# Linear attention and two mixture layers on one core: the first batch's copies, the router's end and the second batch's first unit in another order

## The chip, the core and the metric

The kernel runs on one core of a Trainium2 chip. The core's engines each work through their own list of instructions in order: PE (matrix products), DVE (vector), ACT (activations and copies), POOL (GpSimd), and SP, which issues the transfers (DMAs) and loads a register. An instruction starts when its engine has finished the ones ahead of it in the list and when the results that it needs are there. The metric is the device time of one execution in microseconds (us); lower is better.

## What is computed

```python
q_s = exp(q - max(q, -1));  q_s /= sum(q_s, -1) + 1e-9        # q, k, v: [8 batches, 8 heads, 576 tokens, 64]
k_s = exp(k - max(k, 2));   k_s /= sum(k_s, 2) + 1e-9
x = einsum('bhsd,bhde->bhse', q_s, einsum('bhsd,bhse->bhde', k_s, v))   # then [4608 tokens, 512]
e_idx = argmax(x @ w_gate, 1)                                 # 8 experts
gate = max softmax probability of x @ w_gate
eom = sigmoid(x @ w_output_gate)
for e in range(8):                                            # tokens of expert e
    x2[mask] = gate * eom[:, e] * (relu(x[mask] @ w1[e]) @ w2[e])       # 512 -> 1024 -> 512
h = max(x2 @ m_w1, x2 @ m_w2, x2 @ m_w3)                      # 512 -> 768
out = h @ m_wo
```

## The kernel before

A **unit** is half a batch: four heads of one batch, loaded as k, q and v. Units 0 and 1 are batch 0, units 2 and 3 batch 1, and so on. For a unit the stages are, by the names of the functions: `k_max` (DVE reduces k over a partition's five rows to `kmx`), `k_tr` (PE transposes `kmx` to `kT`; DVE makes `m` and the diagonal `dg`), `k_exp` (PE spreads the maxima to `kB`, DVE subtracts them from `k`, ACT takes the exponential into `ke`), `q_max` (DVE, `qm`), `q_exp` (DVE subtracts, ACT exponential), `q_sum` (DVE: sum `qs`, plus 1e-9, reciprocal), `kv_mm` (PE, k^T v, 20 small products), `kv_norm` (DVE, into `kvraw`, and a store), `q_norm` (DVE, into `qn`), then for each of the unit's two pairs of heads `q_tr` (PE transposes `qn` to `qT`, ACT copies it to `qTf`), `x_mm` (PE, `xT`, copied to `xr` and rounded to the high part in `xs`), `x_lo` (DVE, the low part of `xs`) and `logit_mm` (the router's products, `lgT`).

After a batch's two units the router runs: `logit_tr` and `route_1` choose an expert per token, `route_2` counts and finds the batch's most frequent expert, whose number SP loads into a register; `route_3` makes the tokens' gates; `route_4` and `route_5` make the table of the tokens that belong to other experts. With the number in the register `load_piece` issues the load of that expert's weights: the first piece in four quarters. `split_sub` (ACT) and `split_lo` (DVE for the first two weight tiles, then POOL) split each weight tile into a high and a low part.

The batch then passes through the expert as a whole in 32 **groups**, one per slot: `l1_group` (12 matmuls of 128x288 into `hp`, from `xs` and `w`; ACT writes the high part of `h`, DVE the low part) and `l2_group` (`yp`, from `h` and `w`). Four PSUM buffers (`ps_mm`) hold the groups' results.

The order of everything on every engine is that in which Python emits it. `first` is a list of calls for batch 0 (and some of unit 2, by `in_2`), put in slots -120 and up. From then on `moe_slot` emits a slot's group and then the calls that stand in `events` for that slot. For unit 2 and 3 the slots stand in `EARLY`: ten numbers for `k_max`'s stages in the order of `FRONT` (`None`: not there), and five for each pair in the order of `BACK`; `LOAD` holds the slot in which a unit's loads are issued. Slot 0 has batch 0's first group.

Of the kernel before, what the change touches and what calls it, by code (L numbers as in the profile page):

```python
# [9 lines left out]
F32 = mybir.dt.float32  # L10
F32R = mybir.dt.float32r
I32 = mybir.dt.int32
U32 = mybir.dt.uint32
ACTF = mybir.ActivationFunctionType
# [5 lines left out]
B, H, S, D = 8, 8, 576, 64  # L20
# [8 lines left out]
HF = S // 2  # L29
# [17 lines left out]

STEADY = ((-4, -1, -4, 0, 1, 3, 6, 6, 7, 8), (10, 10, 13, 14, 15), (15, 16, 17, 18, 19))
EARLY = {
    2: ((None, None, None, -8, -5, -3, 0, 0, 3, -1), (2, 3, 3, 7, 5), (5, 6, 7, 8, 9)),  # L50
    3: ((0, 3, 3, 5, 6, 6, 8, 8, 8, 9), (10, 10, 11, 13, 15), (13, 13, 14, 15, 16)),
}
LOAD = {3: -7, 4: 0, 5: 8}
ROUTE = (20, 22)
ROUTE0 = (7, 9)
ROUTE1 = (17, 19)
# [6 lines left out]
def tile_linear_attention__then__moe(  # L63
# [15 lines left out]
    nc = tc.nc  # L79
    dma = nc.sync.dma_start  # L80
    gdma = nc.gpsimd.dma_start
    vec = nc.vector
    act = nc.scalar.activation
# [6 lines left out]
    ident = const.tile([128, 128], F32, name="ident")  # L90
# [33 lines left out]
    x_po = es_x.enter_context(tc.tile_pool(name="x_po", bufs=4))  # L124
    x_pe = es_xe.enter_context(tc.tile_pool(name="x_pe", bufs=4))
# [9 lines left out]
    ps_at = es_att.enter_context(tc.tile_pool(name="ps_at", bufs=1, space=PSUM, side="right"))  # L135
# [49 lines left out]
    units = {}  # L185
    xp = {}
# [55 lines left out]
    def q_inv(b, hb):  # L242
        s = units[b, hb]["qs"]
        vec.tensor_scalar(out=s, in0=s, scalar1=1e-9, scalar2=None, op0=ALU.add)
        vec.reciprocal(out=s, in_=s)

    def q_max(b, hb):
        u = units[b, hb]
        qt = u["q"].rearrange("p h c d -> p (h c) d")
        m = sm.tile([128, 20, 1], F32, tag="qm", name="qm")  # L250
        vec.tensor_reduce(out=m[:, :, 0], in_=qt, axis=AX.X, op=ALU.max)
        u["qm"] = m
# [114 lines left out]
    def x_mm(b, hb, pr):  # L367
        u = units[b, hb]
        g = 2 * hb + pr
        if b == 0:  # L370
            ps = [ps_mm.tile([128, HF], F32, tag="mm", name="xT0") for i in range(2)]
        else:
            big = ps_at.tile([128, 2, 512], F32, tag="big", name="xT")
            ps = [big[:, i, 0:HF] for i in range(2)]
        qT = u["qT", pr]
        for i in range(2):
            cs = slice(HF * i, HF * i + HF)
            if b < NFULL:
                mm(ps[i], kvraw[hb][:, pr], qT[:, 0, cs], start=True, stop=True)
                continue  # L380
            kv = u["kv"]
            for n, (a, c) in enumerate(((0, 0), (0, 1), (1, 0))):
                mm(ps[i], kv[:, a, pr], qT[:, c, cs], start=(n == 0), stop=(n == 2))
        xr = u["xr", pr] = xr_p.tile([128, S], F32, tag="xr", name="xr")
        if b == 0:
            for i in range(2):
                act(out=xr[:, HF * i:HF * i + HF], in_=ps[i], func=ACTF.Copy)
            if hb == 1:
                return
        else:  # L390
            act(out=xr.rearrange("p (a t) -> p a t", a=2), in_=big[:, :, 0:HF], func=ACTF.Copy)
        t = xp[b, g] = (x_po if b % 2 else x_pe).tile([128, 2, S], F32R, tag="x", name="xs")
        act(out=t[:, 0], in_=xr, func=ACTF.Copy)

    def x_lo(b, hb, pr):
        xr = units[b, hb]["xr", pr]
        if b == 0 and hb == 1:
            t = xp[b, 2 * hb + pr] = (x_po if b % 2 else x_pe).tile([128, 2, S], F32R, tag="x", name="xs")
            act(out=t[:, 0], in_=xr, func=ACTF.Copy)
        t = xp[b, 2 * hb + pr]  # L400
        vec.tensor_tensor(out=t[:, 1], in0=xr, in1=t[:, 0].bitcast(F32), op=ALU.subtract)

# [124 lines left out]
    def at(slot, f, *args):  # L527
        events.setdefault(slot, []).append((f, args))
# [4 lines left out]
    def in_2(b, f):  # L533
        f(1, 0)

    first = (
        (load_k, 0), (load_k, 1), (load_q, 0), (load_v, 0), (load_q, 1), (load_v, 1),
        (k_max, 0), (k_tr, 0), (k_max, 1), (k_exp, 0), (k_tr, 1), (q_max, 0), (k_exp, 1), (q_exp, 0),
        (kv_mm, 0), (q_max, 1), (q_sum, 0), (kv_mm, 1), (q_norm, 0), (q_exp, 1), (kv_norm, 0), (q_tr, 0, 0), (kv_lo, 0),
        (load_2,), (q_sum, 1), (q_lo, 0, 0), (q_tr, 0, 1), (x_mm, 0, 0), (kv_norm, 1), (q_lo, 0, 1), (kv_lo, 1),  # L540
        (q_norm, 1), (q_tr, 1, 0), (x_mm, 0, 1), (logit_mm, 0, 0), (q_tr, 1, 1), (x_mm, 1, 0), (logit_mm, 0, 1),
        (x_mm, 1, 1), (x_lo, 0, 0), (x_lo, 0, 1), (logit_mm, 1, 0), (logit_mm, 1, 1), (in_2, q_max), (in_2, k_max),
        (logit_tr,), (route_1,), (route_2,), (in_2, q_exp), (x_lo, 1, 0), (x_lo, 1, 1), (route_3,),
    )
    for i, (f, *a) in enumerate(first):
        at(-120 + i, f, 0, *a)
    at(ROUTE0[0], route_4, 0)
    for c in range(5):
        at(ROUTE0[1] + 2 * c, route_5, 0, c)
    START = {n: 16 * n - 51 for n in range(2, 2 * B)}  # L550
    FRONT = (q_max, q_exp, k_max, k_tr, k_exp, q_sum, kv_mm, kv_norm, kv_lo, q_norm)
    BACK = (q_tr, q_lo, x_mm, x_lo, logit_mm)
    for n, s0 in START.items():
        b, hb = divmod(n, 2)
        if n in EARLY:
            t, s0 = EARLY[n], 0
        else:
            t = STEADY
        if n > 2:
            at(LOAD.get(n, START.get(n - 2, 0) + 9), load_unit, b, hb)  # L560
        for d, f in zip(t[0], FRONT):
# [347 lines left out]
    with tc.manual_schedule():  # L909
# [55 lines left out]
        def out_ps(nm):  # L965
            return ps_o.tile([128, 512], F32, tag="o", name=nm)
# [135 lines left out]
        def fx_kv(b_reg):  # L1102
            kv = fx_p.tile([128, 2, 2, 128], F32, tag="fkv", name="fkv")
            dma(out=kv, in_=kv_d[bass.ds(b_reg, 1)].rearrange("b a p g d -> p (b a) g d"))
            return kv

        def fx_x(kv, qT, qs):
            ps = out_ps("fx")
            for g in range(4):
                mm(ps[:, SLOT * g:SLOT * g + SLOT], kv[:, g // 2, g % 2], qT[:, g, qs], start=True, stop=True)  # L1110
            pv = ps[:, 0:4 * SLOT].rearrange("p (g t) -> p g t", g=4)
            x = fx_p.tile([128, 4, 2, SLOT], F32R, tag="fxs", name="fxs")
            act(out=x[:, :, 0], in_=pv, func=ACTF.Copy)
            vec.tensor_tensor(out=x[:, :, 1], in0=pv, in1=x[:, :, 0].bitcast(F32), op=ALU.subtract)
            return x
# [252 lines left out]
        for c in range(6):  # L1368
# [31 lines left out]
            for i in range(2):  # L1400
                col, x = tiles[i]
# [8 lines left out]
            for i, (col, x) in enumerate(tiles):  # L1410
                m = CAP if x is None else 128
                if i < 2:
                    ps = o[i]
                else:
                    ps = out_ps("op")
# [16 lines left out]
    with tc.For_i(0, n_trip, 1) as it:  # L1432
# [9 lines left out]
        ps = out_ps("lqT")  # L1442
# [6 lines left out]
        x = fx_x(fx_kv(b_reg), qT, slice(0, SLOT))  # L1449
        hh = []  # L1450
        y = None
        for i in range(4):
            ps = out_ps("lm")
# [11 lines left out]
        for f in range(6):  # L1465
# [11 lines left out]
            t = lp.tile([128, SLOT], F32, tag="ltm", name="ltm")  # L1477
# [7 lines left out]
        ps = out_ps("lo")  # L1485
# [40 lines left out]
```

## Time and profile before

| what | value |
|---|---|
| median of three runs | 1200.14 us (1200.04, 1200.14, 1201.42) |
| the profiled execution, its own time | 1197.52 us |
| its span, from the first instruction to the last | 1195.5 us |
| mean granted TensorE clock over the span | 0.986 of full |
| PE busy 45 to 50 us / 50 to 55 us / 55 to 60 us | 0.00 / 4.49 / 5.00 us |
| DVE busy 45 to 50 us / 50 to 55 us / 55 to 60 us | 3.24 / 4.19 / 4.82 us |

The span lies 2.0 us below the execution's own time, and that time lies 2.6 us below the median. PE is busy for 95% of the span; the first expert matmul begins near 50 us. A stretch's clock of 1.00 is 2.4 GHz, of 0.50 it is 1.2 GHz.

### The profile page before, as it was taken

To read this page: it belongs to the slowest core of one execution; us is meant where nothing else is said; L and a number is where in the kernel's file an instruction comes from. 1 tells how busy PE (TensorE), PEld (TensorE's weight loads), DVE (VectorE), ACT (ScalarE), POOL (GpSimd) and SP (SyncE) were. 2 spreads that over 40 slices of the span, in tenths; PEclk is the share of its full clock that TensorE was granted. 3 is DMA by queue.
4 is the path that set the end of the run, shared out by engine and by line. 5 is a ranking of instruction groups with operands and counts; after the bars stand their busy time and mean duration, and the time that the engine had idled before them with its cause. 6 is when DMAs were issued, how large, how long until landed. Compare 5 with 4: busy or idle time off the path is not lost. (4 is left out here: it accounts for less than half of the span.)

```text
span 1195.5 us, 21865 instructions
## 1 busy us (share of the span) xinstructions
PE 1136.8 (95%) x7626; PEld 1061.4 (89%) x7626; DVE 786.4 (66%) x1476; ACT 583.8 (49%) x1549; POOL 412.9 (35%) x502
## 2 busy tenths in 40 slices
PE   4699999999999999999999999999999999999994
PEld 2499899898999999999998899899899989989983
DVE  7777878788787878647798566455556446554430
ACT  2466676756667676536454423443344244333220
POOL 2156857677676857787241020000000000000000
PEclk8799999999999999999999999999999999999997
DMA  6784657576565654437698478487678848747701
GB/s 160 187 226 127 195 156 212 156 221 201 160 193 165 187 143 153 135 137 249 212 320 298 160 236 287 134 295 237 225 231 266 272 147 287 237 138 235 222 19 42
DMA packets 204210, 234.97 MB, mean 197 GB/s; under 512 B 78253, under 2 KB 122061, under 8 KB 204096
## 3 DMA queue, kind: packets, MB, share of 16 engines
q1 hardware_dynamic: 202384, 233.14, 62.7%
q8 instruction: 62, 1.02, 0.4%
q0 software_dynamic: 1712, 0.39, 0.2%
q14 instruction: 52, 0.43, 0.1%
HBM read 189.56 MB, written 44.13 MB: 195 GB/s over the span
## 5 line engine op out<-in xcount | busy, mean ns | idle before, releaser
L668 PE MATMUL yp<-h,w 128*128 128x288 f32 x1536 | 222.7, 299 | 7.4 <-DVE h L656 7.4
L668 PEld LDWEIGHTS yp<-h,w 128*128 128x128 f32 x1536 | 207.7, 188 | 11.4 <-DVE h L656 8.8
L650 PE MATMUL hp<-xs,w 128*128 128x288 f32 x1536 | 217.5, 298 | 0.0
L650 PEld LDWEIGHTS hp<-xs,w 128*128 128x128 f32 x1536 | 206.9, 188 | 2.6
L634 POOL TENSOR_TENSOR w<-stg,w 128x512 fp32r<-128x512 f32 x126 | 180.3, 1436 | 79.6 <-ACT w L627 78.1
L1248 PE MATMUL pY<-t,sw 128*128 128x384 f32 (+1 forms) x972 | 193.5, 342 | 2.1 <-ACT s L1257 1.7
L1248 PEld LDWEIGHTS pY<-t,sw 128*128 128x128 f32 x972 | 172.8, 188 | 6.3 <-ACT s L1257 2.9
L1225 POOL DMA_INDIRECT out_dram<-ocx,ftb x1 | 1.0, 981 | 481.8 <-SPq L1432 481.8
L1336 PE MATMUL op<-wo,hc 128*128 128x512 f32 (+1 forms) x666 | 156.2, 394 | 0.0
L1336 PEld LDWEIGHTS op<-wo,hc 128*128 128x128 f32 (+1 forms) x666 | 125.1, 188 | 27.9
L1257 ACT ACTIVATE s<-pY 128x384 f32<-128x384 f32 (+1 forms) x108 | 53.6, 496 | 133.5 <-PE pY L1248 129.6
L656 DVE SCALAR_TENSOR_TENSOR h<-hp,h 128x288 fp32r<-128x288 f32 x128 | 57.2, 453 | 64.3 <-ACT h L655 62.3
L240 ACT ACTIVATE q<-q,qm 128x64 f32<-128x64 f32 x240 | 80.1, 337 | 0.0
L627 ACT ACTIVATE w<-stg 128x512 fp32r<-128x512 f32 x128 | 78.9, 621 | 0.0
L655 ACT ACTIVATE h<-hp 128x288 fp32r<-128x288 f32 x128 | 50.9, 398 | 40.7 <-PE hp L650 40.5
L1264 ACT ACTIVATE hc<-c 128x384 fp32r<-128x384 f32 (+1 forms) x72 | 38.2, 530 | 62.2 <-DVE c L1287 61.8
L1248 PE MATMUL pZ<-B,sw 128*128 128x384 f32 (+1 forms) x324 | 66.8, 341 | 1.5 <-DVE c L1281 1.5
L1248 PE MATMUL pY<-B,sw 128*128 128x384 f32 (+1 forms) x324 | 66.4, 340 | 0.6 <-DVE y L675 0.6
L1248 PE MATMUL pX<-B,sw 128*128 128x384 f32 (+1 forms) x324 | 66.8, 341 | 0.0
L1248 PE MATMUL pX<-t,sw 128*128 128x384 f32 (+1 forms) x324 | 66.5, 340 | 0.0
L1248 PEld LDWEIGHTS pZ<-B,sw 128*128 128x128 f32 x324 | 57.9, 188 | 3.6 <-DVE c L1281 1.8
L1257 ACT ACTIVATE sx<-pX 128x384 f32<-128x384 f32 (+1 forms) x54 | 26.9, 497 | 67.6 <-PE pX L1248 64.2
(251 smaller groups left out, 1858.7 us busy)
## 6 DMA issues: line engine op xcount, KB each, us to landing
sw<-ws_d SPq DMA_DIRECT2D x315, 256.0 KB, 3.6
stg<-in_moe_w_dram SPq DMA_DIRECT2D x31, 1024.0 KB, 5.3
ws_d<-sw SPq DMA_DIRECT2D x63, 256.0 KB, 3.2
fw<-in_moe_w_dram SPq DMA_DIRECT2D x48, 256.0 KB, 4.1
v<-in_v_dram SPq DMA_DIRECT2D x80, 128.0 KB, 4.7
draw<-in_moe_w_dram SPq DMA_DIRECT2D x24, 384.0 KB, 4.8
k<-in_k_dram SPq DMA_DIRECT2D x16, 512.0 KB, 5.5
q<-in_q_dram SPq DMA_DIRECT2D x16, 512.0 KB, 6.8
```

The source lines that it names most:

```text
L240: act(out=qt[:, i], in_=qt[:, i], func=ACTF.Exp, bias=u["qm"][:, i], accum_out=u["qs"][:, i])
L627: act(out=t[:, 0], in_=src, func=ACTF.Copy)
L634: eng.tensor_tensor(out=t[:, 1], in0=src, in1=t[:, 0].bitcast(F32), op=ALU.subtract)
L650: mm(ps, w[:, a, kk], xp[b, kk][:, c, cs], start=(n == 0), stop=(n == 11))
L655: act(out=h[:, 0, cs], in_=ps, func=ACTF.Relu)
L656: vec.scalar_tensor_tensor(out=h[:, 1, cs], in0=ps, scalar=0.0, in1=h[:, 0, cs].bitcast(F32), op0=ALU.max, op1=ALU.subtract,)
L668: mm(ps, w[:, a, f], ht[f][:, c, cs], start=(n == 0), stop=(n == 11))
L1225: nc.gpsimd.indirect_dma_start(out=out[:, :], out_offset=bass.IndirectOffsetOnAxis(ap=tb[0:n, 0:1], axis=0), in_=src, in_offset=None, boun ...
L1248: mm(ps[:, 0:nn], w[:, a, kap], tt_[key, kap][:, cc, 0:nn], start=(start and k == 0), stop=(k == 5), skip_group_check=True)
L1257: act(out=t[:, 0:n_of(c)], in_=pst[n, "X" if nm == "sx" else "Y"][:, 0:n_of(c)], func=ACTF.Copy)
L1264: act(out=h[:, 0, cols], in_=t[:, 0:nn], func=ACTF.Copy)
L1336: mm(ps[0:m], hc[f][:, a, col:col + m], wo[f][:, cc], start=(f == F_ORDER[0] and i == 0), stop=(f == F_ORDER[5] and i == 2))
```

## The change

For batch 0, `x_mm` no longer makes the high part. A new function `x_hi` does: for unit 0 on POOL, for unit 1 on ACT behind `route_1`. For unit 1 the second half of `xr` is copied by DVE, the first by ACT. In `first`, unit 2's `q_max` stands in front of the low parts, `route_3` and `q_exp` of unit 2 leave the list, unit 2's `k_max` comes behind `route_2`, and `spin` puts 16 transposes of the identity matrix, read by nobody, on PE. `route_3` of batch 0 moves to slot 1. Unit 2's stages get other slots: `q_exp` -4, `k_tr` -6, `k_exp` 0, `q_sum` 1, `q_norm` 2, `kv_mm` and `kv_norm` 3, and its first pair's `q_tr` goes from slot 2 to 3. Unit 4's loads go from slot 0 to 3.

```diff
 EARLY = {
-    2: ((None, None, None, -8, -5, -3, 0, 0, 3, -1), (2, 3, 3, 7, 5), (5, 6, 7, 8, 9)),
+    2: ((None, -4, None, -6, 0, 1, 3, 3, 3, 2), (3, 3, 4, 7, 5), (5, 6, 7, 8, 9)),
-LOAD = {3: -7, 4: 0, 5: 8}
+LOAD = {3: -7, 4: 3, 5: 8}
...
+    def spin(b, n):
+        ps = ps_at.tile([128, 1024], F32, tag="big", name="spin")
+        for i in range(n):
+            nc.tensor.transpose(ps[:, 0:128], ident, ident)
...
             for i in range(2):
-                act(out=xr[:, HF * i:HF * i + HF], in_=ps[i], func=ACTF.Copy)
-            if hb == 1:
-                return
+                if i == 1 and hb == 1:
+                    vec.tensor_copy(xr[:, HF:S], ps[1])
+                else:
+                    act(out=xr[:, HF * i:HF * i + HF], in_=ps[i], func=ACTF.Copy)
+            return
...
+    def x_hi(b, hb, pr):
+        xr = units[b, hb]["xr", pr]
+        t = xp[b, 2 * hb + pr] = x_pe.tile([128, 2, S], F32R, tag="x", name="xs")
+        if hb == 0:
+            nc.gpsimd.tensor_copy(t[:, 0], xr)
+        else:
+            act(out=t[:, 0], in_=xr, func=ACTF.Copy)
...
-        (x_mm, 1, 1), (x_lo, 0, 0), (x_lo, 0, 1), (logit_mm, 1, 0), (logit_mm, 1, 1), (in_2, q_max), (in_2, k_max),
-        (logit_tr,), (route_1,), (route_2,), (in_2, q_exp), (x_lo, 1, 0), (x_lo, 1, 1), (route_3,),
+        (q_norm, 1), (in_2, q_max), (x_hi, 0, 0), (q_tr, 1, 0), (x_mm, 0, 1), (logit_mm, 0, 0), (x_lo, 0, 0),
+        (x_hi, 0, 1), (q_tr, 1, 1), (x_mm, 1, 0), (logit_mm, 0, 1), (x_lo, 0, 1), (x_mm, 1, 1),
+        (logit_mm, 1, 0), (logit_mm, 1, 1), (logit_tr,), (route_1,), (x_hi, 1, 0), (x_hi, 1, 1), (route_2,), (spin, 16),
+        (x_lo, 1, 0), (x_lo, 1, 1), (in_2, k_max),
...
+    at(1, route_3, 0)
```

Line numbers of the changed kernel are 6 to 15 higher than those of before for the same line. The first piece is DVE before, from the first weight tile of batch 0 on. In it `w` is a weight tile's low part, `k`, `qs`, `qn`, `kr` and `kvraw` are unit 2's, `h` is group 0's low part, and `qm` is unit 3's.

```order
L634 TENSOR_TENSOR w<-stg,w 128x512
L281 TENSOR_TENSOR k<-k,kB 128x1280
L634 TENSOR_TENSOR w<-stg,w 128x512
L289 TENSOR_REDUCE qs<-q 128x20
L290 TENSOR_SCALAR qs<-qs 128x20
L291 RECIPROCAL qs<-qs 128x20
L298 TENSOR_TENSOR qn<-q,qs 128x4x5x64
L656 SCALAR_TENSOR_TENSOR h<-hp,h 128x288
L325 TENSOR_SCALAR kr<-kv 128x2
L326 RECIPROCAL kr<-kr 128x2
L329 TENSOR_TENSOR kvraw_202<-kv,kr 64x2x64 x2
L251 TENSOR_REDUCE qm<-q 128x20
```

Unit 2's `qm` and `kmx` (ahead of the router), its subtraction `q` and the six instructions of `route_3` stand above this piece. Next is DVE in the changed kernel, from the low parts of unit 1's `xs` on; `kmx`, `m`, `dg`, `q` and `k` are unit 2's, `h` is group 0's, `qm` is unit 3's.

```order
L414 TENSOR_TENSOR xs<-xr,xs 128x576 x2
L224 TENSOR_REDUCE kmx<-k 128x256
L649 TENSOR_TENSOR w<-stg,w 128x512
L274 TENSOR_REDUCE m_567<-kT 128x2
L277 TENSOR_SCALAR dg<-ident,m_567 128x128 x2
L649 TENSOR_TENSOR w<-stg,w 128x512
L264 TENSOR_TENSOR q<-q,qm 128x1280
L671 SCALAR_TENSOR_TENSOR h<-hp,h 128x288
L287 TENSOR_TENSOR k<-k,kB 128x1280
L257 TENSOR_REDUCE qm<-q 128x20
```

Unit 2's `kmx` and `q` came in here, `h` of group 0 moved ahead of `k`, and unit 3's `qm`, which stood behind unit 2's `kvraw`, stands behind `k`. The rows that follow directly in the changed kernel, from group 1's `h` to unit 2's `qn`:

```order
L671 SCALAR_TENSOR_TENSOR h<-hp,h 128x288
L487 TENSOR_TENSOR rz<-roh,rl 128x40
L489 TENSOR_REDUCE rzs<-rz 128x5
L493 TENSOR_REDUCE rs<-rex 128x5
L494 TENSOR_SCALAR rs<-rs 128x5
L495 SCALAR_TENSOR_TENSOR rs<-rez,rs 128x5
L496 RECIPROCAL tsrc<-rs 128x5
L295 TENSOR_REDUCE qs<-q 128x20
L296 TENSOR_SCALAR qs<-qs 128x20
L297 RECIPROCAL qs<-qs 128x20
L671 SCALAR_TENSOR_TENSOR h<-hp,h 128x288
L304 TENSOR_TENSOR qn<-q,qs 128x4x5x64
```

`route_3` and the low parts of groups 1 and 2 have moved in front of unit 2's `qn`; between the second weight tile and `qn` there stood four instructions, now there stand fifteen. The next piece is PE before, where the expert's groups begin; `hp` x12 is one group, and `kT`, `kB`, `kv` and `qT` are unit 2's.

```order
L266 MATMUL kT<-ident,kmx 128x128 x2
L278 MATMUL kB<-dg,ones 128x256
L650 MATMUL hp<-xs,w 128x288 x12
L316 MATMUL kv<-v_199,ke 64x65 x20
L650 MATMUL hp<-xs,w 128x288 x24
L350 MATMUL qT<-ident,qn 128x128 x4
L351 MATMUL qT<-ident,qn 128x64
L650 MATMUL hp<-xs,w 128x288 x12
```

Here `kv` stands behind one group and `qT` behind three. The same place on PE in the changed kernel:

```order
L251 MATMUL spin<-ident 128x128 x16
L272 MATMUL kT<-ident,kmx 128x128 x2
L665 MATMUL hp<-xs,w 128x288 x12
L284 MATMUL kB<-dg,ones 128x256
L665 MATMUL hp<-xs,w 128x288 x36
L322 MATMUL kv<-v_199,ke 64x65 x20
L356 MATMUL qT<-ident,qn 128x128 x4
L357 MATMUL qT<-ident,qn 128x64
L665 MATMUL hp<-xs,w 128x288 x12
```

`kB` has moved behind group 0 and `kv` behind group 3; `qT`, which stood behind three groups, stands behind four. On SP's list nothing changes place.

## Rows read from the trace of the kernel before

**Rows 1.** Timeline, PE alone: start us, us, work [idle before it <-releaser].
```profile
24.97 1.11 PE L350 MATMUL qT<-ident,qn 128*128 128x128 f32 x4 [3.90 <-DVE qn L298]
...
50.05 1.19 PE L278 MATMUL kB<-dg,ones 128*128 128x256 f32 x2 [8.03 <-DVE dg L271]
50.67 2.98 PE L650 MATMUL hp<-xs,w 128*128 128x288 f32 x12
```

**Rows 2.** Windows: us, busy per engine (x instructions), granted clock, DMA share, GB/s.
```profile
52.50:53.00 0.50, 0.50 (x4) 0.50 (x4) 0.50 (x2) 0.20 (x1) 0.00 (x0) 0.53 1.06 385
```

**Rows 3.** Timeline, DVE alone.
```profile
27.36 0.17 DVE L290 TENSOR_SCALAR qs<-qs 128x20 f32<-128x20 f32 x1
...
36.65 2.36 DVE L224 TENSOR_REDUCE kmx<-k 128x256 f32<-128x1280 f32 x1
...
43.05 1.49 DVE L258 TENSOR_TENSOR q<-q,qm 128x1280 f32<-128x1280 f32 x1
46.44 1.43 DVE L401 TENSOR_TENSOR xs<-xr,xs 128x576 fp32r<-128x576 f32 x2 [1.91 <-ACT xs L399]
47.78 0.19 DVE L474 TENSOR_TENSOR rz<-roh,rl 128x40 f32<-128x40 f32 x1
...
49.00 0.38 DVE L268 TENSOR_REDUCE m<-kT 128x2 f32<-128x256 f32 x1
...
49.82 0.68 DVE L634 TENSOR_TENSOR w<-stg,w 128x512 fp32r<-128x512 f32 x1
51.27 1.49 DVE L281 TENSOR_TENSOR k<-k,kB 128x1280 f32<-128x1280 f32 x1 [0.77 <-PE kB L278]
...
53.28 1.48 DVE L289 TENSOR_REDUCE qs<-q 128x20 f32<-128x1280 f32 x1
54.79 1.18 DVE L290 TENSOR_SCALAR qs<-qs 128x20 f32<-128x20 f32 x1
...
56.32 2.21 DVE L298 TENSOR_TENSOR qn<-q,qs 128x1280 f32<-128x1280 f32 x1
...
59.82 1.49 DVE L251 TENSOR_REDUCE qm<-q 128x20 f32<-128x1280 f32 x1
61.34 1.37 DVE L656 SCALAR_TENSOR_TENSOR h<-hp,h 128x288 fp32r<-128x288 f32 x3
```

**Rows 4.** Timeline, ACT alone.
```profile
36.96 0.90 ACT L387 ACTIVATE xr<-xT 128x288 f32<-128x288 f32 x2 [0.72 <-PE xT L379]
...
44.57 1.27 ACT L259 ACTIVATE q<-q 128x1280 f32<-128x1280 f32 x1 [4.84 <-DVE q L258]
...
48.35 1.13 ACT L627 ACTIVATE w<-stg 128x512 fp32r<-128x512 f32 x2
```

**Rows 5.** Timeline, SP's DMA queue alone.
```profile
43.88 2.10 SPq L609 DMA_DIRECT2D stg<-in_moe_w_dram  x4
...
49.44 2.58 SPq L198 DMA_DIRECT2D q<-in_q_dram  x1
```

**Rows 6.** DMA issues at 27.4, 43.9, 49.4 us: KB each, us to landing.
```profile
q<-in_q_dram SPq DMA_DIRECT2D x1, 512.0 KB, 5.1
...
stg<-in_moe_w_dram SPq DMA_DIRECT2D x1, 256.0 KB, 2.7
...
q<-in_q_dram SPq DMA_DIRECT2D x1, 128.0 KB, 8.8
```

**Rows 7.** Timeline, PE alone, around the first qT of unit 2.
```profile
54.12 1.83 PE L316 MATMUL kv<-v,ke 128*64 128x65 f32 x40 [0.47 <-ACT ke L283]
55.88 3.45 PE L650 MATMUL hp<-xs,w 128*128 128x288 f32 x24
59.17 0.60 PE L350 MATMUL qT<-ident,qn 128*128 128x128 f32 x4
```

**Rows 8.** The page's groups by cost: busy, mean ns | idle before.
```profile
L668 PE MATMUL yp<-h,w 128*128 128x288 f32 x1536 | 222.7, 299 | 7.4 <-DVE h L656 7.4
...
L634 POOL TENSOR_TENSOR w<-stg,w 128x512 fp32r<-128x512 f32 x126 | 180.3, 1436 | 79.6 <-ACT w L627 78.1
```

More of the change, by code (lines that the diff above doesn't have):

```diff
@@ L393, in x_mm @@
         act(out=t[:, 0], in_=xr, func=ACTF.Copy)
+    def x_hi(b, hb, pr):
[5 more added lines that the diff above has]
+            act(out=t[:, 0], in_=xr, func=ACTF.Copy)
     def x_lo(b, hb, pr):
         xr = units[b, hb]["xr", pr]
-        if b == 0 and hb == 1:
-            t = xp[b, 2 * hb + pr] = (x_po if b % 2 else x_pe).tile([128, 2, S], F32R, tag="x", name="xs")
-            act(out=t[:, 0], in_=xr, func=ACTF.Copy)
         t = xp[b, 2 * hb + pr]
@@ L540, in tile_linear_attention__then__moe @@
         (load_2,), (q_sum, 1), (q_lo, 0, 0), (q_tr, 0, 1), (x_mm, 0, 0), (kv_norm, 1), (q_lo, 0, 1), (kv_lo, 1),
-        (q_norm, 1), (q_tr, 1, 0), (x_mm, 0, 1), (logit_mm, 0, 0), (q_tr, 1, 1), (x_mm, 1, 0), (logit_mm, 0, 1),
-        (x_mm, 1, 1), (x_lo, 0, 0), (x_lo, 0, 1), (logit_mm, 1, 0), (logit_mm, 1, 1), (in_2, q_max), (in_2, k_max),
-        (logit_tr,), (route_1,), (route_2,), (in_2, q_exp), (x_lo, 1, 0), (x_lo, 1, 1), (route_3,),
+        (q_norm, 1), (in_2, q_max), (x_hi, 0, 0), (q_tr, 1, 0), (x_mm, 0, 1), (logit_mm, 0, 0), (x_lo, 0, 0),
+        (x_hi, 0, 1), (q_tr, 1, 1), (x_mm, 1, 0), (logit_mm, 0, 1), (x_lo, 0, 1), (x_mm, 1, 1),
+        (logit_mm, 1, 0), (logit_mm, 1, 1), (logit_tr,), (route_1,), (x_hi, 1, 0), (x_hi, 1, 1), (route_2,), (spin, 16),
+        (x_lo, 1, 0), (x_lo, 1, 1), (in_2, k_max),
     )
```

## The prediction

> **What bounds the kernel now.** I read the page's busy shares first, then PE's waits, then the timelines of single engines in the stretch that the change touches. PE is the bound: once the expert's groups have started it hardly ever stands still. So the end moves by as much as PE's list is shifted in the first 70 us, unless something later takes the shift back. Before the groups, PE is idle for long stretches; the last ends when DVE delivers `dg`, after 8.03 us, and the first group then starts at 50.67 [rows 1]. Ahead of that DVE does unit 2's subtraction at 43.05, the low parts of unit 1's `xs` at 46.44 and `route_3` from 47.78 to 49.00, and only then `m`, `dg` and the first weight's low part at 49.82 [rows 3]. From group 0 on PE follows its list with short waits, and unit 2's first `qT` starts at 59.17, behind three groups [rows 7]. That `qT` is the place on which this forecast turns: PE can't pass it before DVE has written `qn`.
>
> **The change, part by part.**
>
> *The copies of batch 0.* ACT waited 0.72 us for PE before its last pair of `xr` copies [rows 4]: it was fed by PE, so its list being shorter gains nothing there. The second copy of that pair now runs on DVE, which could start no earlier than ACT did, since the half that it copies comes from PE last. A DVE copy of 128x288 isn't in the trace; DVE's `h` of the same size takes 0.46 (three in 1.37 [rows 3]), the ACT copy 0.45 [rows 4]. I take no difference; the bounds are 0.45 either way. Unit 2's `qm` now stands ahead of these copies, and its load landed 5.1 us after 27.4 [rows 6], or 32.5, some 4 us before the copies matter. The POOL casts of 128x576 aren't in the trace either: a POOL tile of 128x512 takes 1.44 [rows 8], so some 1.6 by size (an estimate), and the low parts that wait for them are read only after the next groups of PE's list. I cost all of this at nothing; the cover is PE's own chain, and without it each cast would cost its 1.6.
>
> *The first weights.* The first quarter is issued at 43.88 [rows 5] and lands 2.7 us later [rows 6], at 46.6. In the changed kernel nothing stands before ACT's high part (half of 1.13 [rows 4]), which is done at 47.2. DVE, free at 43.05, has `xs` twice (1.43) and `kmx` (2.36) to do [rows 3], until 46.8, then the low part (0.68): the first group starts at about 47.9, 2.8 us earlier than before. The 16 transposes of `spin` cost 16/4 x 1.11 = 4.4 us at the most [rows 1], in a time in which PE waits for `kmx` anyway.
>
> *DVE's list up to unit 2's `qn`.* This pays for it. From 47.9: `m` and `dg` 0.82 (49.00 to 49.82), the second weight 0.68, unit 2's `q` 1.49 [rows 3], so 50.9. Group 0's `h` comes next, and it waits for ACT, which has the exponential of `q` (1.27), two weight tiles (1.13) and the high part of `h` to do first [rows 4]: 53.7. DVE's `h` 0.46, then `k` 1.49 [rows 3]: 55.7. Now comes unit 3's `qm`, and it waits for unit 3's q. The last transfer of that q is issued at 49.44 [rows 5], behind the weights on a list of SP that the change leaves alone, and lands 8.8 us later [rows 6]: 58.2. Before, DVE came to this `qm` at 59.82, when q was there; now it stands 2.6 us, and `route_3`, `q_sum` and `qn` of unit 2 are queued behind it. From 58.24: `qm` 1.52 (59.82 to 61.34), `h` 0.46, `route_3` 1.22, `q_sum` 2.03, `h` 0.46, `qn` 1.49. The 2.03 is 53.28 to 56.32 with the short instruction at 0.17 in place of 1.18; the 1.49 is that of `k`, of the same size [rows 3]. The sum is 7.2 us, so `qn` is done at 65.4.
>
> *PE.* It has four groups, `kB` and `kv` before that `qT`. Even with all four as slow as group 0 was (2.98), `kB` 1.19 [rows 1] and `kv` 1.83 [rows 7], it is through at 62.8; with later groups at 1.65 (55.88 to 59.17 for two [rows 7]) at about 58 to 59. So the clock of the first groups and the head start of 2.8 us are worth nothing, and PE stands some 6 us before `qT`. Before, `qT` came at 59.17 with one group less done, so the shift is 65.4 - 59.17 - 1.65 = 4.6 us.
>
> *The clock after that stop.* Behind 3.90 us of idle time four transposes took 1.11 [rows 1], against 0.60 in `qT` at 59.17 [rows 7]; behind 8.03 us a group took 2.98 in place of 1.65. Work began again at 50.05, and the granted clock rose from 0.50 to 1.00 within the slice 52.5 to 53.0 [rows 2]: 2.9 us at half speed, which loses 1.45. A stop of some 6 us lies between the two; I add 1.5. The bounds are 0 and 1.9 (`qT` and one group at the slow rows: 0.6 + 1.33).
>
> *The rest:* unit 4's loads and the store of `kvraw` ahead of them keep their places among SP's transfers; they come later with `kvraw`, by about what PE's list does, and I cost them at nothing of their own. The bound is that shift itself, if what reads them has no slack.
>
> The sum is 4.6 + 1.5 = 6.1 us. The profiled execution took 1197.52 around its span of 1195.5, so 1203.6 for one like it; the median of the runs lies 2.62 higher, which gives 1206.2.
>
> *POOL beside DVE.* While POOL split weight tiles, DVE's short instruction took 1.18 in place of 0.17 and `qn` 2.21 in place of 1.49 [rows 3]. If both happen again `qn` is 1.7 us later. I take 0 for the sum, since POOL gets few tiles while DVE stands still (a POOL tile follows ACT's high part, and ACT's list holds its fifth tile behind `ke` and its sixth behind group 2's high part), and keep 1.7 for the range. The Trainium skill's page "SBUF — State Buffer", section "SBUF: two separate sides", says why: a vector instruction with two inputs in SBUF, or in a two-port mode, and a GpSimd instruction shut each other out for a whole instruction, whoever starts first; reductions never do. By that rule only the sixth tile, at about 62 to 63.4, can be met, by the short instructions, for about 0.4 us (an estimate from that page and the POOL row), and the forecast would be 1206.6.
>
> **The rivals.**
>
> *POOL holds DVE as it did before:* +1.7, 1207.9. For it: it did so in this very stretch. Against: the tiles come later now.
>
> *Unit 3's q is no obstacle* (it lands by 55.7): `qn` at 62.9, a shift of 2.0, and 3.5 with the slow clock: 1202.2 to 1203.7. Against it stands the landing, 58.2, on a list of transfers that isn't altered.
>
> *The shift is given back later* (not slower): PE waits 7.4 us in all for DVE's `h` before the second products [rows 8]. If DVE's lists there ran by their own time and not by PE's, a PE that comes 6.1 later would wait up to 6.1 less, and the time would be 1200.1. It decides from 3.7 us given back. Against it: an `h` is made from a group's product, so DVE in those places moves with PE.
>
> *The head start is kept* (faster): then `qn` must be done by 59.17 + 1.65 = 60.8, and the kernel would take 1200.14 - 2.8 = 1197.3. Without the wait for ACT (2.8) and the wait for q (2.6) `qn` would come at 60.0 and gain 0.8 at most; both waits would have to be wrong.
>
> **How the numbers follow.** The sum as worked out: 0.60, between 1204.7 (no slow clock) and 1208.4 (POOL, and 1.9 for the clock). POOL's rival 0.12, q's 0.08, the shift given back 0.13, the head start kept 0.07. A change of under 0.2% (2.4 us, 1197.7 to 1202.5) is about what a measurement of this kernel can't tell from none. Slower by more: 0.60 + 0.12, half of q's rival and a small part of the shift given back, 0.78. Within: 0.15. Faster: 0.07. The range 1200 to 1209 leaves out the head start, some half of the shift given back, and a little above.
>
> **What would show it.** In the profile of the changed kernel: the first `hp` at about 48 and four groups in a row; DVE idle for some 2.8 us before group 0's `h` (ended by ACT) and some 2.6 before unit 3's `qm` (ended by a DMA); `qn` done at 65 to 67; PE's longest wait after the first group before unit 2's `qT`, ended by DVE's `qn`, some 6 us; a granted clock of 0.50 in some of the 4 us behind it; the first `yp` some 6 us later than before, by the same list. The forecast is wrong if unit 3's q lands well before 58, if `qT` starts before 61, or if PE's later waits for `h` shrink by more than 3 us.

## The result, and the profile after

The changed kernel takes 1209.08 us, median of 6 runs (1207.45 to 1212.31), beside 1200.09 (1198.06 to 1203.23, 6 runs) for the kernel before: a ratio of 1.0077, 95% interval 1.0057 to 1.0097, or 9.0 us slower. A second series of each gave 1207.98 against 1199.01 (1.0074). Slower was forecast; the size was 6.1 us, and 1209.08 lies just above the range's end of 1209. The profiled execution took 1207.94 around a span of 1205.9.

PE's timeline after, which answers to [rows 1] and [rows 7] (start us, us, work [idle before it <-releaser]):

```profile
41.13 3.42 PE L251 MATMUL spin<-ident 128*128 128x128 f32 x16
46.28 0.45 PE L272 MATMUL kT<-ident,kmx 128*128 128x128 f32 x2 [1.73 <-DVE kmx L224]
47.03 2.96 PE L665 MATMUL hp<-xs,w 128*128 128x288 f32 x12 [0.30 <-ACT w L642]
49.78 1.05 PE L284 MATMUL kB<-dg,ones 128*128 128x256 f32 x2
50.28 5.76 PE L665 MATMUL hp<-xs,w 128*128 128x288 f32 x36
56.52 1.83 PE L322 MATMUL kv<-v,ke 128*64 128x65 f32 x40 [0.49 <-ACT ke L289]
65.01 1.12 PE L356 MATMUL qT<-ident,qn 128*128 128x128 f32 x4 [6.66 <-DVE qn L304]
66.05 0.37 PE L357 MATMUL qT<-ident,qn 64*128 64x64 f32 x1
66.35 2.91 PE L665 MATMUL hp<-xs,w 128*128 128x288 f32 x12
...
77.65 1.57 PE L683 MATMUL yp<-h,w 128*128 128x288 f32 x9
```

The wait of 8.03 us ahead of the first group is gone, and the first group starts 3.6 us earlier (47.03 against 50.67). Behind four groups and `kv` PE stands 6.66 us for `qn`. The first second product starts at 77.65, before at 71.73: 5.92 later.

DVE's timeline after, for [rows 3]:

```profile
53.31 0.46 DVE L671 SCALAR_TENSOR_TENSOR h<-hp,h 128x288 fp32r<-128x288 f32 x1 [2.68 <-ACT h L670]
53.69 1.48 DVE L287 TENSOR_TENSOR k<-k,kB 128x1280 f32<-128x1280 f32 x1
58.32 1.49 DVE L257 TENSOR_REDUCE qm<-q 128x20 f32<-128x1280 f32 x1 [3.15 <-DMA q<-in_q_dram]
...
62.70 0.23 DVE L296 TENSOR_SCALAR qs<-qs 128x20 f32<-128x20 f32 x1
...
63.47 1.48 DVE L304 TENSOR_TENSOR qn<-q,qs 128x1280 f32<-128x1280 f32 x1
```

Both waits of the forecast are there: 2.68 us for ACT, then 3.15 us for unit 3's q, which lands at 58.3, with unit 2's `q_sum` and `qn` queued behind it. POOL doesn't hold DVE up (0.23 and 1.48 us, where [rows 3] has 1.18 and 2.21).

Windows after, for [rows 2] (the granted clock is the third number from the end):

```profile
60.00:65.00 5.00, 0.00 (x0) 0.00 (x0) 4.72 (x13) 1.32 (x4) 1.26 (x1) 0.69 0.55 204
65.00:70.00 5.00, 4.99 (x22) 4.39 (x22) 4.89 (x7) 2.33 (x3) 0.00 (x0) 0.63 0.49 141
70.00:75.00 5.00, 5.00 (x43) 4.45 (x43) 1.91 (x6) 2.81 (x5) 2.39 (x7) 1.00 1.14 250
```

During the stop the granted clock falls, and the work that resumes at 65.01 runs in part at the lower of the two levels (1.2 GHz); from 70 on it is at the upper (2.4 GHz). POOL's two copies, which the trace of before didn't have:

```profile
31.33 0.66 POOL L407 CAST xs<-xr 128x576 fp32r<-128x576 f32 x1 [8.22 <-ACT xr L396]
33.37 0.67 POOL L407 CAST xs<-xr 128x576 fp32r<-128x576 f32 x1 [1.38 <-ACT xr L396]
```

So up to 78 us the program went as forecast. But its end is 10.4 us later than in the first profile of the kernel before (spans 1205.9 and 1195.5), not 5.9. The page's groups after, for [rows 8], show some of it as waits: PE stands for `h` 8.0 us ahead of second products (7.4 before), and 1.0 ahead of a first product, where there was nothing.

```profile
L683 PE MATMUL yp<-h,w 128*128 128x288 f32 x1536 | 224.6, 301 | 8.0 <-DVE h L671 8.0
L665 PE MATMUL hp<-xs,w 128*128 128x288 f32 x1536 | 219.4, 299 | 1.4 <-DVE h L671 1.0
```

Another part is a fall of the clock to 0.50 (1.2 GHz) behind a PE wait of 1.76 us, at the start of a batch's second products, where 26 matmuls take 5.23 us instead of 3.71. PE's timeline after, then windows after:

```profile
221.65 5.23 PE L683 MATMUL yp<-h,w 128*128 128x288 f32 x26 [1.76 <-DVE h L671]
```

```profile
219.00:221.00 2.00, 0.89 (x6) 0.49 (x4) 1.97 (x2) 1.79 (x5) 2.00 (x2) 1.00 0.48 162
221.00:223.00 2.00, 1.35 (x8) 1.35 (x9) 2.00 (x5) 0.79 (x2) 1.57 (x3) 0.83 0.88 187
223.00:225.00 2.00, 2.00 (x10) 2.00 (x10) 1.66 (x2) 0.14 (x1) 2.00 (x3) 0.50 1.08 350
```

### The profile page after: what moved, and what is told of

It reads as the page before. It is cut to its first block, busy times and chain, and to the rows that moved or that the text cites. A ratio compares the mean times of both kernels' runs of the same rounds, so it can differ in the third digit from the quotient of the medians.

```text
span 1205.9 us, 21901 instructions
## 1 busy us (share of the span) xinstructions
PE 1145.8 (95%) x7642; PEld 1068.0 (89%) x7642; DVE 785.6 (65%) x1478; ACT 580.9 (48%) x1545; POOL 411.1 (34%) x504
## 5 line engine op out<-in xcount | busy, mean ns | idle before, releaser
L1263 PEld LDWEIGHTS pX<-B,sw 128*128 128x128 f32 x324 | 57.6, 188 | 2.4 <-issue 0.7
```

Source lines behind the costliest of these rows:

```text
L1263: mm(ps[:, 0:nn], w[:, a, kap], tt_[key, kap][:, cc, 0:nn], start=(start and k == 0), stop=(k == 5), skip_group_check=True)
```

## The experiments

The question was where the 3 us behind the first second product come from. The first theory was that the list's shift is carried to the end one to one, so that its size must have been misread; its rival, that something later adds to it. A third, late theory was that an edit priced at nothing is the cause.

**Unit 3's q maximum three slots later** (the changed kernel; takes away the wait for q).

```diff
-    3: ((0, 3, 3, 5, 6, 6, 8, 8, 8, 9), ...
+    3: ((3, 3, 3, 5, 6, 6, 8, 8, 8, 9), ...
```

> The changed kernel with unit 3's qm moved from slot 0 to slot 3, behind unit 2's qn; nothing else. Theory A (DVE stood 3.15 us for unit 3's q, and unit 2's qn and PE's qT stood behind it): DVE goes on at 57.3 with group 1's h, qn is done near 62.7, qT starts near 62.8 in place of 65.0, and the first yp near 75.4 in place of 77.65. The time is 2.2 us under that of the changed kernel, some 1206.9. Rival B (the wait for q only fills a time in which DVE would wait for ACT or for weights): qT stays within 0.5 us of 65.0 and the time within 0.5 us of 1209.

1206.56 us (1.0058, 1.0042 to 1.0073), 7.5 over its runs of the kernel before (1199.09), where the change was 9.0 over its own. DVE's timeline in it has no wait for q, but a new one in its place, for a group's high part on ACT, and `route_3` with 1.65 us instead of 1.22 behind it:

```profile
57.81 0.46 DVE L671 SCALAR_TENSOR_TENSOR h<-hp,h 128x288 fp32r<-128x288 f32 x1 [2.15 <-ACT h L670]
```

`qT` starts at 63.63 instead of 65.01, where the first theory had 62.8, and the first second product comes 1.0 earlier (76.68). The wait was real, but taking its 3.15 us away brings 1.4 on the path. That the time lies close to the 1206.9 of that theory therefore doesn't prove it.

**The copies alone** (the kernel before with `x_hi`, the half copy by DVE and the new places of the low parts; nothing else moved, no `spin` issued).

```diff
-        (x_mm, 1, 1), (x_lo, 0, 0), (x_lo, 0, 1), (logit_mm, 1, 0), ...
+        (q_norm, 1), (x_hi, 0, 0), (q_tr, 1, 0), (x_mm, 0, 1), (logit_mm, 0, 0), (x_lo, 0, 0), ...
```

> The kernel before with the copies of batch 0 alone (POOL and ACT high parts in x_hi, DVE's half of xr); unit 2 and the router's end stand where they stood before. Theory A: the router's number comes 0.46 us earlier, as it did in the changed kernel, and the low parts of unit 1's xs no longer wait behind ACT's exponential (1.91 us in the kernel before), so dg and the first group come 1.5 to 2 us earlier than at 50.67: some 1198.3. Rival B (the first prediction's: the copies are worth nothing): 1200.1. Neither expects it slower; if it is, the copies are part of the loss.

1200.56 us over 12 runs, 1.0007 (0.9992 to 1.0021): no difference that can be measured.

**PE busy through the stop** (the changed kernel with 40 more idle transposes at slot 3).

```diff
+    at(3, spin, 0, 40)
```

> The changed kernel with 40 more transposes of the identity on PE, in front of unit 2's kv, so that PE is busy for some 6.3 of the 6.66 us in which it stood still. Theory A (the restart at the lower clock cost 1.5 to 1.7 us): qT still at 65.0, the granted clock stays 1.00 behind it, the next group takes 1.85 in place of 2.91, the first yp comes near 76.0, and the time is 1.7 us under that of the changed kernel, near 1207.4. Rival B (the clock behind the stop is worth nothing, since DVE is late there anyway): the first yp at 77.6 and 1209.

1207.1 us (1.0068, 1.0049 to 1.0086). The transposes keep the clock: `qT` takes 0.63 us instead of 1.12. But unit 3's q lands later in that profile (DVE waits 3.96 us for it, until 59.63), `qT` starts at 66.41, and the first group behind it takes 3.25 us all the same. The first second product stands at 78.91, 1.3 later than in the changed kernel. The 1.5 us of the clock couldn't be had by that, and a time close to the first theory's 1207.4 is no proof of it.

**A pure delay of PE, early** (the kernel before with 40 idle transposes at slot 2).

```diff
+    at(2, spin, 0, 40)
```

> The kernel before with 40 transposes of the identity in front of unit 2's first qT: PE and all that follows it is held up by some 6.2 us at 59 us, with the clock kept up, and nothing else is changed. Theory A (a shift at the first yp is carried to the end as it is, and what the changed kernel lost beyond 5.9 us is chance of the runs): the time is 6.2 us over that of the kernel before, 1206.3. Rival B (a late PE loses more later on, in the waits for h and in the clock behind them): some 3 us more than the delay, 1209. Rival C (the shift is given back later): under 1204.

1209.52 us (1.0081, 1.0065 to 1.0097), against 1199.09: 10.4 us, though in its profile the first second product stands only 5.0 later. So a list that is shifted by 5 us, with nothing of the change in it, also ends some 10 later. One to one is wrong, or the transposes cost more than their time.

**The q sum early again** (the changed kernel with `q_sum` and `kv_mm` one slot earlier, `route_3` at slot 5, unit 2's `q_exp` ahead of its `k_max`, unit 3's `q_max` at slot 3).

```diff
-    2: ((None, -4, None, -6, 0, 1, 3, 3, 3, 2), ...
+    2: ((None, None, None, -6, 0, 0, 2, 3, 3, 1), ...
-        (x_lo, 1, 0), (x_lo, 1, 1), (in_2, k_max),
+        (x_lo, 1, 0), (x_lo, 1, 1), (in_2, q_exp), (in_2, k_max),
-    at(1, route_3, 0)
+    at(5, route_3, 0)
```

> The change with four further edits: unit 2's q sum and k^T v one slot earlier, the router's third step from slot 1 to slot 5, unit 2's exponentials of q ahead of its k maximum, and unit 3's q maximum from slot 0 to slot 3. Same computation. Walked by the order of the queues with the durations of the profile of the changed kernel: the last sum over q is ready at about 57.1 instead of 64.9, PE's transpose of q starts at about 58.2 without a wait, and the first second product at about 69.1, that is 2.6 us ahead of the kernel before and 8.5 us ahead of the change. Theory A (what stands at the first second product is kept to the end, and the 3 us that the changed kernel lost later are chance of single runs): 1196.5 to 1198. Theory B (the kernel before meets the later steady state in a favourable place, and any displacement, early or late, is followed by clock falls worth about 3 us): 1199 to 1202. Theory C (the lead is lost to the later waits for transfers that are not tied to PE): 1199 to 1200.5, with longer PE waits where the trace of before has short ones.

1204.93 us (1.0046, 1.0029 to 1.0064), outside what any of the three theories had given. `qT` starts at 58.42 without a wait, as walked, but the next waits come right behind it. PE's timeline:

```profile
58.42 0.60 PE L356 MATMUL qT<-ident,qn 128*128 128x128 f32 x4
...
65.65 0.52 PE L424 MATMUL lgT<-xr,wgt 128*32 128x128 f32 x10 [2.08 <-ACT xr L399]
...
70.25 0.67 PE L284 MATMUL kB<-dg,ones 128*128 128x256 f32 x2 [1.34 <-DVE dg L277]
```

DVE is full with unit 3's q and k from 60.45 to 65.7; ACT's copy of x is queued behind unit 3's exponential, and the first second product stands 1.4 us later than before instead of 2.6 earlier. Even so the time is 4.8 later, 3.4 more than that.

**A pure delay of PE, late** (the kernel before with 40 idle transposes at slot 102).

```diff
+    at(102, spin, 0, 40)
```

> The kernel before with 40 idle transposes of 128 columns (about 4.4 us of PE, 40 by 0.11 us) put into PE's list at slot 102, at about 245 us, instead of slot 2 at about 60 us. Theory A (a pure delay is carried one to one, wherever it stands): before plus 4.4, 1203.5 to 1204.5. Theory B (any displacement costs a few us more behind it): before plus 7 to 9, 1206.5 to 1208.5, with a stretch of lower granted clock or added PE waits behind the place. Theory C (only a delay in the first hundred microseconds grows, since the first batches' transfers and the decoding's loads are placed against it): before plus 4 to 5.5, and the early delay stays at plus 9 to 10.

1205.07 us (1.0050, 1.0032 to 1.0068): 5.0 us, though in the profile PE's list is 2.6 us later behind the place (0.3 ahead of the profile of before at 238 us, 1.9 to 2.5 behind it from 306 to 443). The transposes stand at 277.45 us there, not near 245, and take 4.53 us; the 1.28 us for which PE waits behind that place in the profile of before are gone. By its time alone this is theory C, but set against what the list was shifted, the late delay grew as well.

**Both kernels profiled once more.**

> The kernel before, profiled once more. If the first profile was one of its faster runs by chance (1197.52 against a median near 1199.5), this one shows 1 to 2 us more, and the clock fall of 1.5 us behind a PE wait near 1.8 us, which the first profile lacks and all other profiles have once. If the fall belongs to displaced kernels alone, it is absent again.

> The changed kernel, profiled once more. If the growth after the first second product is the placing of waits in one run, the shift at the first second product is again 5.9 and the later steps (0.4 at 90, 1.6 at 222, 1.2 by the end) stand at other places or are missing. If they belong to the changed kernel, they recur at the same places.

The kernel before took 1202.67 this time, 5.15 more than in its first profile. 4.0 of it arise in one place, between 238 and 306 us, where its first profile has a wait of 1.28 us and no fall; this one has waits of 1.11 and 1.75 us and a fall. PE's timeline, and windows:

```profile
285.20 6.49 PE L668 MATMUL yp<-h,w 128*128 128x288 f32 x26 [1.75 <-DVE h L656]
```

```profile
286.00:288.00 2.00, 2.00 (x10) 2.00 (x9) 1.64 (x3) 0.93 (x2) 2.00 (x2) 0.50 1.07 349
288.00:290.00 2.00, 2.00 (x10) 2.00 (x10) 1.93 (x3) 0.54 (x2) 1.43 (x2) 0.50 0.98 297
```

So falls of the clock at a batch's first second products belong to both kernels and come and go between runs. The changed kernel, at 1209.99, had its first second product 7.68 later, its fall at 290 us instead of 222, and again a wait of 0.75 us for `h` near 570 us. A single pair of profiles doesn't size the growth; medians must.

**The changed kernel without its idle transposes.** They are 16 transposes that nobody reads, issued while PE waits for unit 2's `kmx`.

```diff
-        ... (route_2,), (spin, 16),
+        ... (route_2,),
```

> The changed kernel without its 16 idle transposes of PE ahead of the first weights. Theory A (the time follows what stands at the first second product, and later waits add 2 to 4 us to any list of the changed order): the first group may start at a lower granted clock, but PE idles 6.7 us behind it anyway, so the transpose of q stays at 65.0 and the time within 1 us of the changed kernel, 1208 to 1210. Theory D (the later growth comes from the longer list of PE instructions, which all kernels that grew have and the kernel before and the one with the copies alone have not): 1205.5 to 1207, and no PE wait for h near 570 us.

1206.58 us (1.0057, 1.0041 to 1.0073). The first product starts at 46.95 and the first second product stands 5.6 later, as with them; the time is 6.6 later than before, not 9.0. That is theory D by the time; its other sign failed, since PE waits 0.98 us for `h` near 570 us here too.

**Head start, rebalanced** (unit 3's `q_max`, `q_exp` and `q_sum` later, `route_3` behind unit 3's `k_tr`).

```diff
-    3: ((3, 3, 3, 5, 6, 6, 8, 8, 8, 9), ...
+    3: ((4, 6, 3, 5, 6, 7, 8, 8, 8, 9), ...
```

> The kernel with the head start, with unit 3's q moved behind: its maximum at slot 4, its exponentials at slot 6, its sum at slot 7, its k maximum in front at slot 3, and the router's third step behind unit 3's k transposes. In the head start's profile PE idled 2.1 us for the copy of x, held on ACT behind unit 3's exponentials, and 1.3 us for the diagonal, held on DVE. Walked with its durations: no wait for the copy, the first second product at 69.5 to 70.5 against 71.73 before. Theory A: the shift at the first second product is -1.2 to -2.2, the late part adds 2 to 4, so 1199 to 1202 against a median before of 1200. Rival E (DVE is full between 52 and 72 us, so the wait moves to unit 3's sum over q a few slots on): 1203 to 1205.5, with a PE wait of 1.5 to 3 us for qn between 74 and 82 us.

1205.12 us over 12 runs (1.0049, 1.0032 to 1.0066). Both waits are gone and the first second product is 1.7 us ahead of before, at 70.01; then PE stands for unit 3's `qn`, as rival E had it:

```profile
80.94 0.63 PE L356 MATMUL qT<-ident,qn 128*128 128x128 f32 x4 [2.63 <-DVE qn L304]
```

**The order alone** (the changed kernel with batch 0's copies by ACT as before).

```diff
-                if i == 1 and hb == 1:
-                    vec.tensor_copy(xr[:, HF:S], ps[1])
-        (q_norm, 1), (in_2, q_max), (x_hi, 0, 0), (q_tr, 1, 0), ...
+        (q_norm, 1), (in_2, q_max), (q_tr, 1, 0), ...
```

> The changed kernel with the copies of the first batch as before (ACT alone, four at once), so the change's order without its copies. If the order carries the whole loss, as the copies alone measured nothing (1.0007): 1208 to 1210.5. If the copies by three engines gave back something that the order alone would lose: 1210.5 to 1213. If copies and order only together collide (POOL's copies with DVE): 1203 to 1206.

1209.42 us (1.0086, 1.0067 to 1.0104): the order, with the 16 transposes that this kernel still has, carries the whole loss, the copies none.

**Idle transposes alone** (the kernel before with 16 of them, ahead of unit 2's `kT`).

```diff
-        ... (in_2, q_exp), (x_lo, 1, 0), ...
+        ... (in_2, q_exp), (spin, 16), (x_lo, 1, 0), ...
```

> The kernel before with 16 idle transposes of PE ahead of unit 2's k transposes, in a place where PE then idles 8 us for DVE's diagonal. They delay nothing. Theory A: same time as before, 0.999 to 1.0015, no PE wait for h near 570 us. Theory D (a longer list of PE instructions alone shifts the later transfers and costs 2 to 3 us): 1.0015 to 1.003, with the wait near 570 us. A third outcome: the transposes keep the granted clock up for the first group (2.98 us at a low clock before), and the time falls by about 1 us.

1201.9 us over 12 runs (1.0018, 1.0004 to 1.0032). PE's timeline: they take 2.88 us out of a wait that then still lasts 5.14, and the first group starts no later than before (50.42 against 50.67). The first second product is 0.55 later; near 567 us there is a wait for `h` that no profile of the kernel before has.

```profile
41.34 2.88 PE L250 MATMUL spin<-ident 128*128 128x128 f32 x16
44.02 0.63 PE L271 MATMUL kT<-ident,kmx 128*128 128x128 f32 x2
49.80 1.19 PE L283 MATMUL kB<-dg,ones 128*128 128x256 f32 x2 [5.14 <-DVE dg L276]
50.42 3.44 PE L655 MATMUL hp<-xs,w 128*128 128x288 f32 x12
...
567.13 8.15 PE L655 MATMUL hp<-xs,w 128*128 128x288 f32 x48 [1.91 <-DVE h L661]
```

**With and without them on one chip; at the start; doubled.** The first two are the changed kernel and the one without its transposes once more; the third is the kernel before with `(spin, 16)` as the first entry behind the loads, the fourth with `(spin, 32)` where the run above has 16.

> The changed kernel once more, to stand beside the next one on the same chip. If the idle transposes cost 2 to 3 us: 1208 to 1210, 1.0065 to 1.009, apart from the next. If the difference was scatter between chips and runs: the same as the next.

> The changed kernel without its 16 idle transposes once more. If they cost 2 to 3 us: 1206 to 1207.5, the 6.1 us of the sum plus at most 1. If they cost nothing: 1208 to 1210 as with them.

> The kernel before with the 16 idle transposes at the start of the program, where PE waits for the first k and nothing depends on them. Theory D1 (a longer list of PE instructions shifts the later course): 1201 to 1203, a PE wait for h of 1 to 2.5 us near 570 us. Theory D2 (their place in front of the first weights matters): the same as before, no such wait. If there was never a cost: also the same as before.

> The kernel before with 32 idle transposes instead of 16 in front of unit 2's k transposes, still within the 8 us in which PE idles there. Theory D1 by number: 1203 to 1205, twice the cost of 16. Theory D3 (any further length tips the late stretch once): as with 16, 1201 to 1203. If there was never a cost: the same as before.

| kernel | median us (runs) | to before | 95% interval |
|---|---|---|---|
| changed | 1207.98 (6) | 1.0074 | 1.0057 to 1.0091 |
| changed, no transposes | 1204.81 (7) | 1.0043 | 1.0026 to 1.0059 |
| before, 16 at the start | 1201.66 (12) | 1.0016 | 1.0004 to 1.0028 |
| before, 32 | 1203.04 (11) | 1.0039 | 1.0026 to 1.0052 |

At the start PE waits for the first k, and the first second product is 0.08 us off its place of before; the cost is there nonetheless. Their place in front of the first weights doesn't matter. Between the changed kernel and the one without them the medians lie 3.2 us apart here, and the two intervals just touch. Put together with the earlier runs of the same two kernels, the means lie 3.4 us apart, with a 95% interval of 1.5 to 5.3 (worked out from the times of these runs, each less those of its kernel before).

**Idle instructions on DVE instead** (the kernel before with 32 small writes that nobody reads, as many instructions as 16 transposes with their weight loads).

```diff
+    def idle_dve(b, n):
+        z = sm.tile([128, 8], F32, tag="zz", bufs=1, name="zz")
+        for i in range(n):
+            vec.memset(z, 0.0)
...
+        (idle_dve, 32), (k_max, 0), (k_tr, 0), ...
```

> The kernel before with 32 small idle writes on DVE (about 0.06 us each) at the start, before the first k has landed, instead of 16 idle transposes on PE (32 instructions of PE). If a longer list of any engine costs: 1.0015 to 1.004, 1201.5 to 1204. If it is PE's list (or PE's work) alone: the same as before, 0.9988 to 1.0012.

1199.66 us (0.9998, 0.9989 to 1.0007): nothing. A longer list of just any engine isn't what costs; it is a matter of PE, though the runs don't tell PE's list from PE's work. The first second product stands 1.2 us later in this profile (72.93), and in the second profile of the kernel before 0.6 later (72.32): places scatter by that much from one profile to the next.

**The q sum early, without the transposes.**

> The kernel with the head start without its 16 idle transposes. There the first second product stood 1.4 us later than before and the time was 4.8 later. If the two causes add up (place of the first second product, plus 2 to 3 for the transposes): 1201 to 1202.5, 1.0008 to 1.0022. If the head start's other rearrangements cost by themselves: 1203.5 to 1205.5, as with them.

1201.07 us over 12 runs (1.0020, 1.0008 to 1.0033), 2.4 us by the ratio and 1.55 by the medians; its first second product stands 1.8 later than before. That is what the two causes added up had given, 1201 to 1202.5. In the three profiles of the changed order without transposes the time keeps within about 1 us of the list's shift: 5.6 became 6.6 and 6.9 became 5.8 (the two runs of the changed kernel without them), 1.8 became 1.6.

## Why the prediction was right, and where it failed

**The shift was right, step by step.** First weights: issued at 43.41 (43.88 taken), first group at 47.03 (47.9). DVE's wait for ACT: 2.68 (2.8). Landing of unit 3's q: 58.3 (58.24), a wait of 3.15 (2.6). `qn` done at 64.95 (65.4), PE's stop 6.66 (some 6), first second product 5.92 later (6.1, clock included). Of the two terms, the shift at `qT` was 65.01 - 59.17 - 1.65 = 4.2 us (4.6), which leaves 1.7 for the clock (1.5). The landing was met partly by luck: the last piece of that q was issued at 50.29, 0.85 later than taken, and took 8.0 us instead of 8.8; with 40 more transposes it landed 1.3 us later. The copies cost nothing, as forecast, shown by the run with them alone and the one without them. POOL's casts took 0.66, not 1.6.

**The step that failed** is the price of `spin`: "in a time in which PE waits for `kmx` anyway" was taken to mean that the 16 transposes cost nothing. They do lie in that time (41.13 to 44.55, and `kT`, which needs `kmx`, starts at 46.28), and still the kernel is 2.4 and 3.2 us faster without them (6.6 and 5.8 over the kernel before, in place of 9.0 and 9.0, by the medians). The first pair alone isn't clear of noise, the two together are. Alone, in the kernel before, they cost 1.9 us by the medians (1.0018) in one place and 2.6 (1.0016) in another. The sum of the forecast, 6.1 us, lies between the two that the kernel without them measures. So the mechanism of the shift held, and the term put at nothing measured 2 to 3 us. By what path it reaches the end stays open.

**The other sentence that doesn't hold** is that the end moves by just the list's shift "unless something later takes the shift back". With PE's further instructions it moved by more in most runs: 5.0 became 10.4, 2.6 became 5.0, 1.4 became 4.8; with PE busy through the stop, 7.2 became only 8.0.

**The rivals.** POOL holding DVE: it didn't (`qn` 1.48), so that its 1207.9 came close is chance. Unit 3's q no obstacle: refuted by the wait of 3.15; yet its price was put too high, since taking the wait away moved `qT` by 1.4, with ACT's group 1 next in line. The shift given back: refuted, PE's waits for `h` grew from 7.4 to 8.0. The head start kept: it was lost in the 6.66, and in both rearranged kernels the lead was lost within a dozen slots, to DVE's list and in the first of them also to ACT's. No version tried beats the kernel before.

**What stays open** is how transposes in idle time cost 2 to 3 us later on. Every profile of a kernel with them has a PE wait for DVE's `h` at one place near 570 us, 0.4 us in the doubled one and 0.75 to 2.66 in the twelve others. Of the seven without, six have 0.1 or nothing and one has 1.0. The page's groups of the kernel with 16 at the start, and of the one with idle writes on DVE:

```profile
L655 PE MATMUL hp<-xs,w 128*128 128x288 f32 x1536 | 218.3, 299 | 2.0 <-DVE h L661 2.0
```

```profile
L655 PE MATMUL hp<-xs,w 128*128 128x288 f32 x1536 | 217.6, 298 | 0.0
```

In the kernels with 16 alone this wait is about as long as what they cost (1.91 and 1.98 us), and in four of the thirteen profiles a fall of the clock follows it (48 matmuls in 8.1 to 8.2 us instead of 6.6). But it is 0.4 us of the 4.0 that 32 cost, and 0.75 to 1.0 in the changed kernel, which lost 2 to 3 by its transposes, so it can't be the whole cost. The traces lead one step further back: DVE's work ahead of this `h` hangs on ACT's rounding of `B`, and that waits for `yr`, the expert's stored result that is loaded back for the second layer. ACT's timeline in the same two kernels:

```profile
550.23 0.53 ACT L907 ACTIVATE B<-yr 128x384 fp32r<-128x384 f32 x1 [0.79 <-DMA yr<-y_d]
```

```profile
547.45 0.53 ACT L907 ACTIVATE B<-yr 128x384 fp32r<-128x384 f32 x1
```

The first `B` waits 0.28 to 1.44 us for that load in eleven of the thirteen profiles with transposes, and in one of the seven without (0.72, the one with the wait of 1.0). Why PE meets this load earlier, and what links that to instructions issued 500 us before, isn't shown. The page counts one more transfer of instructions (63 against 62) in the kernels with transposes, but with 32 it is 63 too, so the count doesn't follow the price. How the price goes with the number isn't settled either: 32 cost about twice what 16 did, and 40 in front of unit 2's `qT` cost 5.4 over their delay, but 40 at slot 102 cost 2.4 over theirs, and the changed kernel with 56 measured 8.0, no more than with 16.

## What to carry to other kernels

When a stage is pulled ahead on the engine that bounds the kernel, look for the next thing that engine needs from the loaded helper engine: here 3.6 us gained at the first group were lost behind the fourth, because the sum over q stood on DVE behind an `h` that waited 2.68 us for ACT and an instruction that waited 3.15 us for the load of the next unit; taking away the second wait alone brought only 1.4. Don't price filler work at nothing because its engine is idle at that moment; take it out and time the kernel without it. And size what comes behind the change by medians of several runs, since two profiles of one and the same kernel here lie 5 us apart.

## What the hardware showed that was not expected

- Sixteen transposes that nobody reads, on a PE that waits, cost 1.9 and 2.6 us (1.0018 and 1.0016) in two places before the first group, and 32 cost 4.0 (1.0039); 32 idle writes on DVE cost nothing (0.9998).
- A PE wait of 1.75 us for `h` may or may not be followed by the lower clock: in the kernel before, one at 285 us was followed by 26 matmuls in 6.49 us (granted clock 0.50 from 286 to 290); in the order alone, one of the same length at 223 us by 26 in 3.71 (clock 1.00 from 221 to 227).
- A POOL cast of 128x576 took 0.66 us, less than half of what its tile subtractions (1.44 for 128x512, [rows 8]) suggested.
